# Weight sums of the next layer's projection: other queues, an earlier place, and one part on another engine

## The chip, the core and the metric

The kernel runs on one core of one Trainium2 chip. A core has a matrix engine (TensorE, in the profile PE, its weight loads PEld), three engines for elementwise work (VectorE, DVE; ScalarE, ACT; GpSimd, POOL), and SyncE (SP), which here only issues DMAs. Each of the five works through its own instructions in order; they wait for one another by semaphores. DMAs are issued by SyncE, ScalarE and Pool, each on a queue of its own, and are carried by 16 DMA engines.

The metric is the device time of one execution in microseconds, lower is better. A profiled execution comes with it, whose times are counted from the first instruction.

## What is computed

Two layers, each an attention block and a gated block with layer norms in front; both layers use the same weights. S is 2048 tokens, D is 448 features, 16 heads of 28, F is 1792, all in float32:

```python
def _A_ref(x, wqkv, wo):
    B, S, D = x.shape
    H = 16
    Dh = D // H
    qkv = (lambda x, *d: x.transpose(*d))((x @ wqkv).reshape(B, S, 3, H, Dh), 2, 0, 3, 1, 4)
    q, k, v = qkv[0], qkv[1], qkv[2]
    scores = jnp.einsum("bhqd,bhkd->bhqk", q, k) * (Dh ** -0.5)
    p = _softmax(scores, axis=-1)
    o = jnp.einsum("bhqk,bhkd->bhqd", p, v)
    return (lambda x, *d: x.transpose(*d))(o, 0, 2, 1, 3).reshape(B, S, D) @ wo

def _B_ref(x, w_gate, w_up, w_down):
    g = jnp.einsum("bsd,df->bsf", x, w_gate)
    u = jnp.einsum("bsd,df->bsf", x, w_up)
    h = _sigmoid(g) * u
    return jnp.einsum("bsf,fd->bsd", h, w_down)

x = A_x
x = x + _A_ref(_layernorm(x, axis=-1), A_wqkv, A_wo)
x = x + _B_ref(_layernorm(x, axis=-1), B_w_gate, B_w_up, B_w_down)
x = x + _A_ref(_layernorm(x, axis=-1), A_wqkv, A_wo)
x = x + _B_ref(_layernorm(x, axis=-1), B_w_gate, B_w_up, B_w_down)
```

## The kernel before

Tokens are worked on in four blocks of 512. Products are made in float16 with every operand split in a high and a low part, so that three products (high by high, high by low, low by high) stand for one in float32. The high part is a scaled copy, the low part the rest, and the two parts of an activation are usually made by ScalarE (high) and VectorE (low).

**What the weight sums are for.** From the second layer on, part of the query and key projection is made by a scheme with fewer multiplications. It needs sums and differences of 2 x 2 sub-blocks of the weights. These are made once, during the first layer, kept in device memory (`qs_parts`), and loaded again at the end of the first layer. The columns of the query and key weights are 7 tiles of 128; three pairs of them, `PAIRS_QK = ((0, 1), (4, 5), (2, 6))`, are treated this way. For each pair there are two steps:

- `read_pair(j, queue)` (L725) reads the pair's columns with four DMAs (for each of the two tiles one of 384 rows and one of 64 rows, L731 and L732) into half of a tile `raws`, and has Pool zero the rows left over (L733). Pairs 0 and 1 share one `raws`.
- `keep_pair(j)` (L738) makes the sums: `add_up` (L246, L254) four additions on VectorE; `split_sums` (L257) then four high parts, on ScalarE (L263) or, if it is handed VectorE, there (L261), and six low parts on VectorE (L266), into a tile `pack`; Pool then writes it to `qs_parts` by a DMA (L748). Where the two tiles of the pair have different scales (pair 2), VectorE scales both first (L744).

**Storage.** Tiles in fast memory come from a list of 19 slots (`big`) that is first in, first out: `get` takes the slot free the longest, `put` hands one back at the end. A new tile waits until the last work on its slot's previous tile is done, a DMA included. A second list (`qrt`, 12 slots) holds the small ones.

**The first layer's projection** (`project`, L823). For each block, `qk` makes the seven query and key tiles: 11 matmuls each (L618) into one of four rotating banks; ScalarE makes the high part (L868), VectorE the low part (L869), ScalarE the squares (L871), VectorE the first step of their maximum (L875), and SyncE writes both parts to device memory (L878). The product that adds up the squares of a head (L847, L850) is issued three tiles late. After the eviction of tile i comes whatever stands in `fill[i]`. After the seven tiles, `vals` makes four value products (L643 to L641), evicted by ScalarE (L1119); `after[j]` is called before the eviction of value tile j.

The blocks' normalised rows go through device memory to be transposed: `squares` (L362, L379) on VectorE, `store` (L391, four DMAs on SyncE), `gather` (L399, L401, SyncE, which waits until the store has landed), then `ready` (L222 ScalarE, L223 VectorE) splits the gathered features in two parts. `tell.add` (L1297) measures other weights on VectorE during blocks 2 and 3.

Pair 0 is read on SyncE's queue during the value products of block 1, after block 3's gather, and kept in `fill[0]` of block 2. Pair 1 is read on SyncE's queue in `fill[0]` of block 3, and kept at the end of `guard_of_norms` (L1215), which is called during the value products of block 2 and prepares the bound for the softmax. Then comes a branch on that bound (L1241) and the attention.

**Attention and what follows.** `attend` (L1495) runs some 450 us with TensorE, ScalarE and VectorE together; pair 2 is read near its end on Pool's queue (`along`). `out_project` (L1683) multiplies with `wo`: after the products of six token tiles VectorE does `keep_pair(2)`, then adds the first four results to x (L1709) and takes their statistics (L549, L550). Pool makes the factor of the norm from them (L552, L554), VectorE scales the rows with it (L362), TensorE turns them (L562). Ahead of this, ScalarE issues four DMAs, loads the table of the next function (L1685) and then makes pair 2's high parts.

Of the kernel before, what the change touches and what calls it, by code (L numbers as in the profile page):

```python
# [121 lines left out]
def interleaved_layers(ctx: ExitStack, tc: tile.TileContext, x_in, wqkv, wo, w_gate, w_up,  # L122
                       w_down, out):
    nc = tc.nc
# [29 lines left out]
    def bank(i, name):  # L154
        return psum(f"bank{i}", name, [P, 512])
# [101 lines left out]
    def split_sums(t, v, by, engine=None):  # L257

        def high(to, a):
            if engine is nc.vector:  # L260
                nc.vector.tensor_scalar(to, a, by, None, op0=ALU.mult)  # L261
            else:
                nc.scalar.activation(to, a, AF.Copy, scale=by)  # L263

        def low(to, hi, a):
            nc.vector.scalar_tensor_tensor(to, a, by[0:hi.shape[0]], hi, op0=ALU.mult,  # L266
                                           op1=ALU.subtract)

        sums = add_up(v)
        s12, s34 = [a.rearrange("p a k n -> p (a k) n") for a in sums]  # L270
        for to, a in ((t[:, 0:2], v[:, 0:2, 0]), (t[:, 2:6], s12), (t[:, 6:10], s34),
                      (t[:, 10:14].rearrange("p (k z) n -> p k z n", k=2), v[:, 2:4])):
            high(to, a)
        for to, hi, a in ((t[:, 14:16], t[:, 0:2], v[:, 0:2, 0]),
                          (t[:, 16:20], t[:, 2:6], s12),
                          (t[:, 20:23], t[:, 6:9], s34[:, 0:3]),
                          (t[:, 23:25], t[:, 10:12], v[:, 2])):
            low(to, hi, a)
        low(t[64:P, 9], t[0:64, 9], s34[0:64, 3])
        low(t[64:P, 12:14], t[0:64, 12:14], v[0:64, 3])  # L280
        qrt.put(*sums)
# [373 lines left out]
    class WeightsQKV:  # L655
# [79 lines left out]
        def pair(self, j):  # L735
            return self.raws[:, j % 2].rearrange("p (s z n) -> p s z n", s=4, z=2)

        def keep_pair(self, j):  # L738
            v, t = self.pair(j), big.get("pack", [P, N_SUMS, P], F16)
            m = [int(i > ALONE) for i in PAIRS_QK[j]]  # L740
            by = up[:, m[0]:m[0] + 1]
            if m[0] != m[1]:
                for z in range(2):
                    nc.vector.tensor_scalar(v[:, :, z], v[:, :, z], up[:, m[z]:m[z] + 1], None,  # L744
                                            op0=ALU.mult)
                by = ones[:, 0:1]
            split_sums(t, v, by)
            nc.gpsimd.dma_start(qs_parts[j], t)  # L748
            big.put(t)
            if j > 0:  # L750
                big.put(self.raws)
# [71 lines left out]
    def project(layer, wq, begun):  # L823
# [4 lines left out]
        def ones_of_values():  # L828
            for v in values:
                nc.gpsimd.memset(v[:, :, :, DH:VC], 0.0)  # L830
                nc.gpsimd.memset(v[:, :, :, DH:DH + 1], 1.0)
# [313 lines left out]
        blks = begun + [Block(b, layer == 1, True) for b in range(len(begun), NB)]  # L1145
        idle = None
        sq = lambda b, *js: lambda: blks[b].squares(js)
        b1, b2, b3 = blks[1:]
        if layer == 0:
# [12 lines left out]
            fill = [idle, idle, lambda: b1.norm([0, 1]), lambda: b1.norm([2, 3]), idle, scaled]  # L1162
# [5 lines left out]
        if layer == 0:  # L1168
            fin = qk(0, blks[0], fill, None)
            vals(0, blks[0], along_values)  # L1170
            fill = [b2.gather, b3.norm, sq(3, 0, 1), sq(3, 2, 3), idle,
                    lambda: b2.ready(0, 1), lambda: (b2.ready(2, 3), b3.store())]
            fin = qk(1, b1, fill, None)
            vals(1, b1, {0: b3.gather, 1: lambda: wq.read_pair(0), 2: fin})
            add = tell.add
            fin = qk(2, b2, [lambda: wq.keep_pair(0),
                             lambda: b3.ready(0, 1), lambda: b3.ready(2, 3), idle, add, add,
                             add], None)
            fin = qk(3, blks[3], [lambda: (add(), wq.read_pair(1)), add, add], fin)
        else:  # L1180
            ones_of_values()
            wq.load_usual()
            h2, h3, s3 = b2.half_steps(), b3.half_steps(), b3.squared()
            ready = [lambda kt=kt: b1.ready(kt) for kt in range(4)]
            both = lambda *steps: lambda: [do() for do in steps]
            fin = qk_sums(0, blks[0], {0: ready[0:1], 1: ready[1:2], 2: s3[0:1],
                                       4: ready[2:3], 5: ready[3:4] + s3[1:2]})
            vals(0, blks[0], {0: both(s3[2], s3[3], s3[6], h2[0]), 1: both(s3[4], s3[7]),
                              2: both(fin, s3[5], s3[8], s3[9], b3.store),
                              3: both(h2[1], h2[2], b3.gather)})  # L1190
            fin = qk(1, b1, h2[3:10], None)
            big.put(*wq.qk)
            vals(1, b1, {0: both(*h3[0:2]), 1: both(h3[2], fin), 2: both(*h3[3:5]),
                         3: h3[5]}, banks=(3, 0, 1, 6))
            fin = qk_sums(2, b2, {0: h3[6:7], 1: h3[7:8], 3: h3[8:9], 4: h3[9:10]}, None, True)
            fin = qk_sums(3, b3, {}, fin)
# [18 lines left out]
        def guard_of_norms():  # L1215

            fin()
            heads[0].load()
            nc.vector.tensor_reduce(top, peaks, axis=AX.X, op=ALU.max)
            nc.vector.scalar_tensor_tensor(bnd, top[:, 0:1], SLACK, top[:, 1:2], op0=ALU.mult,  # L1220
                                           op1=ALU.mult)
            nc.gpsimd.tensor_tensor(bnd, bnd, half[0:H, 0:1], op=ALU.pow)
            nc.vector.tensor_scalar(guard, zero, bnd, -1.0 / UNIT, op0=ALU.add, op1=ALU.mult)
            nc.gpsimd.dma_start(g_scr[:, 0, :], guard)
            nc.gpsimd.dma_start(g_scr[:, 1, :], zero)
            big.put(guard, zero)
            if layer == 0:
                wq.keep_pair(1)

        def worst_of_heads():  # L1230
            pb = bank(4, "bounds")
            nc.tensor.matmul(pb[0:1, 0:H], bnd, ident[0:H, 0:H], start=True, stop=True)
# [450 lines left out]
    def out_project(outs, gate, wq):  # L1683
        new_banks()
        nc.scalar.activation(warm, warm, AF.Sigmoid)  # L1685
        nc.scalar.reg_load(gate_scale, back.bitcast(I32)[0:1, 3:4])
        first, second = Block(0, True), Block(1, True)
        steps = deque([first.turn_raw] + first.half_steps())
        early = second.squared()[:TB + TB // 2]
        pms = {}  # L1690

        def products(ts, banks):
            for t, i in zip(ts, banks):
                pms[t] = bank(i, "op")[:, 0:D]
                by_tokens(pms[t], outs.hi(t), outs.lo(t), None, gate.out, range(3))

        def tails(ts):


            for t in ts:  # L1700
                nc.tensor.matmul(pms[t], outs.tail(t), gate.out[:, 0, 3, :], start=False,  # L1701
                                 stop=False)
            for i, t in enumerate(ts):
                r = slice(64 * (i % 2), 64 * (i % 2) + 64)
                nc.tensor.matmul(pms[t], outs.tail(t, i % 2), gate.out[r, 1, 3, :], start=False,  # L1705
                                 stop=True)

        def add(t):
            nc.vector.scalar_tensor_tensor(x[:, t, :], pms[t], back[:, 1:2], x[:, t, :],  # L1709
                                           op0=ALU.mult, op1=ALU.add)  # L1710

        gate.load_gu()
        gate.load_usual()
        products(range(6), range(6))
        if wq:
            wq.keep_pair(2)
        first.begin()
        tails(range(4))
        for t in range(4):
            add(t)  # L1720
            first.stats(t)
        products((6, 7), (6, 7))
        tails(range(4, 8))
        for t in range(4, 8):
            add(t)
        for t in range(4):
            first.scale(t)
        products((8, 9), (0, 1))
        products((10,), (6,))
        run_fill(steps)  # L1730
        for do in early[:2]:
            do()
        products((11,), (7,))
        run_fill(steps, 2)
        tails(range(8, 12))
        for t in range(8, 12):
            add(t)
        for do in early[2:]:
            do()
        products((12, 13), (2, 3))  # L1740
        run_fill(steps, 4)
        products((14, 15), (0, 1))
        run_fill(steps, 9)
        tails(range(12, NT))
        for t in range(12, NT):
            add(t)
        big.put(*outs.kt, gate.out)
        return first, second
# [425 lines left out]
    wq = WeightsQKV()  # L2174
# [44 lines left out]
    for layer in range(LAYERS):  # L2219
# [4 lines left out]
        wq = WeightsQKV()  # L2224
# [30 lines left out]
```

## Time and profile before

| | |
|---|---|
| three runs, us | 1907.41, 1908.41, 1908.43 |
| median of the runs | 1908.41 us |
| the profiled execution's own time | 1906.35 us |
| its span, first to last instruction | 1904.6 us |
| mean granted clock of TensorE | 0.997 |
| data moved by DMA | 278.71 MB |

In the profile's timelines a row is: start in us, length in us, engine, line of the kernel, operation, output <- inputs, shapes, how many instructions are merged in the row, and in brackets how long the engine stood idle before it and what ended that. `SPq`, `ACTq`, `POOLq` and `DVEq` are the queues' own instructions, such as issuing a DMA. In a view of waits a row has the total in us, the number of times, and the longest. In a view of one source line a row has the least, median and longest duration in ns, and the first and last start. In a view by windows a row has the stretch, then for each engine its busy time, then the granted clock, the busy share of the DMA engines and what they moved in GB/s.

### The profile page before, as it was taken

Reading aid. Unit: us, or ns where it says so; the run is one execution under the profiler, and the core shown is the slowest. Engines: PE = TensorE matmul, PEld = TensorE weight load, DVE = VectorE, ACT = ScalarE, POOL = GpSimd, SP = SyncE. Lnnn points to the kernel's source line nnn. Section 1 sums busy time; section 2 is a strip of 40 time slices with the busy share of each in tenths; the row PEclk is TensorE's granted clock in tenths of the full one; section 3 lists DMA queues with packets and bytes.
Section 4 is the critical chain, followed back from the end, with each engine's and each line's share of the span. In section 5 each row is a group of like instructions: output and inputs, shape, how many; then the busy total and the mean of one; then the engine's idle time right before and its main releaser. Section 6 shows DMA issues by size and latency. Waiting matters only on the chain. (4 is left out here: it accounts for less than half of the span.)

```text
span 1904.6 us, 57187 instructions
## 1 busy us (share of the span) xinstructions
PE 1883.3 (99%) x24531; PEld 1365.9 (72%) x24531; DVE 1479.3 (78%) x2984; ACT 1424.6 (75%) x1885; POOL 248.8 (13%) x481
## 2 busy tenths in 40 slices
PE   9899999999999999999999999999999999999999
PEld 4446755556554899999987565687656668999998
DVE  7668989898987887777867577787787688877664
ACT  5459999999993665555547799999999746555541
POOL 3123112122201111212110000000000021111110
PEclk9999999999999999999999999999999999999999
DMA  7666434434332755556583421221120246566553
GB/s 249 205 196 191 141 108 137 115 113 131 109 116 82 239 195 212 213 205 224 195 254 117 117 51 29 49 51 40 38 52 13 74 151 229 198 230 223 215 207 141
DMA packets 118872, 278.71 MB, mean 146 GB/s; under 512 B 14574, under 2 KB 74478, under 8 KB 118480
## 3 DMA queue, kind: packets, MB, share of 16 engines
q0 software_dynamic: 33296, 165.13, 24.0%
q1 hardware_dynamic: 84160, 108.45, 20.1%
q8 instruction: 194, 3.18, 0.7%
q10 hardware_dynamic: 1152, 1.38, 0.3%
q14 instruction: 70, 0.57, 0.1%
HBM read 213.43 MB, written 53.08 MB: 140 GB/s over the span
## 5 line engine op out<-in xcount | busy, mean ns | idle before, releaser
L1538 ACT ACTIVATE prob_s<-sc 128x1536 f32<-128x1536 f32 (+1 forms) x657 | 888.2, 1483 | 8.9 <-PE sc L1523 8.0
L1574 PE MATMUL acc<-prob_s,val_s 128*32 128x256 f32 (+3 forms) x7700 | 574.8, 384 | 0.2 <-issue 0.2
L1523 PE MATMUL sc<-qp_s 114*32 114x512 f16 x7868 | 557.8, 379 | 0.1
L633 PEld LDWEIGHTS <-gu_s 128*128 128x128 f16 x4368 | 426.7, 98 | 45.9 <-PE op L1705 0.7
L1523 PEld LDWEIGHTS <-qp_s 114*32 114x32 f16 x8192 | 282.1, 96 | 195.3 <-issue 83.3
L1574 PEld LDWEIGHTS acc<-prob_s,val_s 128*32 128x32 f32 x7700 | 283.1, 110 | 132.1 <-issue 12.3
L633 PE MATMUL chain<-xwide_s,gu_s 128*128 128x256 f16 x2016 | 247.6, 273 | 0.0
L1887 PE MATMUL dnp<-dn_s,hparts_s 128*128 128x224 f16 x2184 | 246.0, 259 | 0.3 <-DVE x L1905 0.3
L1887 PEld LDWEIGHTS <-hparts_s 128*128 128x128 f16 x2184 | 210.2, 98 | 5.6 <-issue 0.5
L1554 DVE SCALAR_TENSOR_TENSOR power_q<-power_q,expo_q 128x512 f32<-128x512 f32 x243 | 168.2, 692 | 8.3
L1960 ACT COPY one_q<-chain 128x256 f32<-128x256 f32 x224 | 82.3, 372 | 113.2 <-PE chain L633 112.6
L1976 DVE TENSOR_TENSOR one_q<-side,one_q 128x512 f32<-128x512 f32 x112 | 72.2, 686 | 96.5 <-PE side L633 96.4
L633 PE MATMUL side<-xshort_s,gu_s 128*128 128x256 f16 x1120 | 140.6, 273 | 0.0
L1768 POOL DMA_DIRECT2D gu_s<-gu_parts x104 | 56.2, 541 | 427.4 <-PE side L633 426.0
L1605 DVE STREAM_TRANSPOSE oturned_q<-acc 128x512 f32<-128x512 f32 x32 | 23.0, 717 | 98.4 <-PE acc L1574 98.3
L1840 ACT CAST hparts_s<-hsums_q 128x256 f16<-128x256 f32 (+1 forms) x152 | 71.5, 484 | 36.6 <-DVE hsums_q L1852 23.0
L1574 PE MATMUL acc<-power_q,val_s 128*32 128x256 f32 (+3 forms) x300 | 94.2, 396 | 0.0
L633 PE MATMUL side<-xwide_s,gu_s 128*128 128x256 f16 x672 | 91.7, 273 | 0.0
L618 PE MATMUL qkp<-xhl_s,wqk_s 128*128 128x512 f16 x385 | 88.9, 386 | 0.9 <-ACT wqk_s L235 0.6
L1987 ACT ACTIVATE one_q<-one_q 128x512 f32<-128x512 f32 x56 | 35.3, 630 | 65.2 <-DVE one_q L1976 64.9
L1548 DVE TENSOR_SCALAR expo_q<-aside,base 128x512 f32<-128x512 f32 x81 | 60.6, 748 | 21.8 <-PE aside L1523 21.5
L1844 DVE TENSOR_TENSOR hparts_s<-hsums_q,hparts_s 128x256 f16<-128x256 f32 (+1 forms) x152 | 72.7, 517 | 5.9 <-ACT hparts_s L1840 5.9
(262 smaller groups left out, 2398.1 us busy)
## 6 DMA issues: line engine op xcount, KB each, us to landing
gu_s<-gu_parts POOLq DMA_DIRECT2D x104, 800.0 KB, 5.9
dn_s<-dn_parts POOLq DMA_DIRECT2D x42, 784.0 KB, 7.5
qp_s<-qk_scr SPq DMA_DIRECT2D x96, 224.0 KB
gu_parts<-pack_s POOLq DMA_DIRECT2D x14, 800.0 KB, 3.8
xt_scr<-xs_s SPq DMA_DIRECT2D x48, 224.0 KB
xraw_s<-xt_scr SPq DMA_DIRECT2D x12, 768.0 KB
qk_scr<-qkhl_q SPq DMA_DIRECT2D x35, 256.0 KB
qp_s<-qk_scr SPq DMA_DIRECT2D x64, 112.0 KB
```

The lines of the kernel that those rows point to most:

```text
L618: nc.tensor.matmul(pm, w, x, start=(i == 0), stop=(i == len(terms) - 1))
L633: nc.tensor.matmul(pm, a, x, start=(first and i == 0), stop=(i == len(terms) - 1), skip_group_check=True)
L1523: nc.tensor.matmul(ps[32 * j:32 * j + 32, :], hd.k[:, keys], hd.q[:, qb * W:(qb + 1) * W], start=True, stop=True, tile_position=(0, 32 * j))
L1538: nc.scalar.activation(prob[:, 0:n, :], ps[:, 0:n, :], AF.Exp, scale=exp_scale)
L1548: nc.vector.tensor_scalar(y, ps, base2[:, 0:1], -126.0, op0=ALU.mult, op1=ALU.max)
L1554: nc.vector.scalar_tensor_tensor(p, p, c[k], y, op0=ALU.add, op1=ALU.mult)
L1574: nc.tensor.matmul(acc[qb * VC:(qb + 1) * VC, s], v[:, kc % TB, h, :], probs[c * NB + qb][:, s], start=(kc == 0 and a == 0), stop=(kc == N ...
L1840: nc.scalar.copy(to[:, :, 0], a)
L1844: nc.vector.tensor_tensor(to[:, :, 1], a, to[:, :, 0], op=ALU.subtract)
L1887: nc.tensor.matmul(pm, a[:, x, t], w[:, p, y], start=(begin and n == 0 and (j == 0 or alone)), stop=(n == 2), skip_group_check=True)
L1960: nc.scalar.copy(to, pm)
L1976: nc.vector.tensor_tensor(one[m], side[m], one[m], op=ALU.add)
```

## The change

Pair 0 is read on Pool's queue in `fill[2]` of block 1, between the two halves of block 3's `squares`; pair 1 on ScalarE's queue at the second value tile of block 1, where pair 0 was read. Pair 0 is kept before the first tile of block 2, pair 1 after it. The read of pair 1 in block 3 and its keeping in `guard_of_norms` are gone. Pair 2 is kept where it was, and its high parts are made by VectorE.

```diff
-        def keep_pair(self, j):
+        def keep_pair(self, j, engine=None):
...
-            split_sums(t, v, by)
+            split_sums(t, v, by, engine)
...
-            fill = [b2.gather, b3.norm, sq(3, 0, 1), sq(3, 2, 3), idle,
+            fill = [b2.gather, b3.norm,
+                    lambda: (b3.squares([0, 1]), wq.read_pair(0, nc.gpsimd)), sq(3, 2, 3), idle,
                     lambda: b2.ready(0, 1), lambda: (b2.ready(2, 3), b3.store())]
             fin = qk(1, b1, fill, None)
-            vals(1, b1, {0: b3.gather, 1: lambda: wq.read_pair(0), 2: fin})
+            vals(1, b1, {0: b3.gather, 1: lambda: wq.read_pair(1, nc.scalar), 2: fin})
+            wq.keep_pair(0)
             add = tell.add
-            fin = qk(2, b2, [lambda: wq.keep_pair(0),
+            fin = qk(2, b2, [lambda: wq.keep_pair(1),
                              lambda: b3.ready(0, 1), lambda: b3.ready(2, 3), idle, add, add,
                              add], None)
-            fin = qk(3, blks[3], [lambda: (add(), wq.read_pair(1)), add, add], fin)
+            fin = qk(3, blks[3], [add, add, add], fin)
...
             big.put(guard, zero)
-            if layer == 0:
-                wq.keep_pair(1)
-
         def worst_of_heads():
...
         if wq:
-            wq.keep_pair(2)
+            wq.keep_pair(2, nc.vector)
         first.begin()
```

## The prediction

> **What bounds the kernel.** I read the engine totals first, then what TensorE waited for over the whole run, since an engine that is busy 99% of the span can only be helped where it stands still.
>
> ```profile
> PE 1883.3 (99%) x24531; PEld 1365.9 (72%) x24531; DVE 1479.3 (78%) x2984; ACT 1424.6 (75%) x1885; POOL 248.8 (13%) x481
> ...
> PE qnorm L847 <- DVE sq_q L875: 6.9, 1, 6.9
> PE turn L562 <- DVE xn_s L362: 4.9, 2, 3.6
> PE vp L643 <- DVEq L1241: 1.9, 1, 1.9
> PE op L643 <- DVE x L1709: 0.9, 1, 0.9
> ```
>
> Two places matter: one stall of 6.9 us, and one group of 0.9 + 3.6 us. The change touches the cause of both. The timelines of TensorE, SyncE, ScalarE and VectorE around the first (start, length, engine, line) show it:
>
> ```profile
> 77.46 2.54 PE L618 MATMUL qkp<-xhl_s,wqk_s 128*128 128x512 f16 x11
> 86.90 0.37 PE L847 MATMUL qnorm<-sq_q,ind 128*128 128x256 bf16 x1 [6.90 <-DVE sq_q L875]
> 87.06 4.82 PE L618 MATMUL qkp<-xhl_s,wqk_s 128*128 128x512 f16 x11
> 91.72 0.27 PE L847 MATMUL qnorm<-sq_q,ind 128*128 128x256 bf16 x1
> 111.92 0.35 PE L643 MATMUL vp<-wv_s,xhl_s 128*128 128x448 f16 x1
> ...
> 74.02 0.38 SPq L399 DMA_DIRECT2D xraw_s<-xt_scr  x1
> 74.99 0.58 SPq L731 DMA_DIRECT2D raws_s<-in_A_wqkv_dram  x1
> 76.79 0.50 SPq L732 DMA_DIRECT2D raws_s<-in_A_wqkv_dram  x1
> ...
> 80.60 0.51 ACT L263 ACTIVATE pack_s<-raws_s,up 128x256 f16<-128x256 f32 x1 [8.91 <-DMA raws_s<-in_A_wqkv_dram]
> ...
> 81.63 0.42 DVE L254 TENSOR_TENSOR sums_q<-raws_s 128x256 f32<-128x256 f32 x1 [9.61 <-DMA raws_s<-in_A_wqkv_dram]
> 85.45 0.47 DVE L266 SCALAR_TENSOR_TENSOR pack_s<-raws_s,up,pack_s 64x256 f16<-64x256 f32 x1
> 86.56 0.28 DVE L875 TENSOR_TENSOR sq_q<-sq_q 128x256 bf16<-128x256 bf16 x1
> 88.57 0.28 DVE L875 TENSOR_TENSOR sq_q<-sq_q 128x256 bf16<-128x256 bf16 x1
> 108.52 0.28 DVE L875 TENSOR_TENSOR sq_q<-sq_q 128x256 bf16<-128x256 bf16 x1
> ```
>
> Pair 0 stands on SyncE's queue behind block 3's gather, which waits until block 3's store has landed (74.02). So its read is issued at 74.99 to 77.29 and used from 80.60. ScalarE and VectorE work in order, and the pair's sums stand ahead of the eviction of tile 1 of block 2. Tile 1's squares are ready at 86.84; TensorE had finished tile 4 at 80.00 and needs them for the norm product. After the gap 11 matmuls take 4.82 us and not 2.54. The place costs 6.9 + 2.3 = **9.2 us**.
>
> **The change, first stage.** Pair 0's four issues go to Pool's queue during block 1, pair 1's four to ScalarE's queue; both pairs' sums then stand around tile 0 of block 2, and guard_of_norms and SyncE's queue lose pair 1. I followed the first-in-first-out slot list through the code: pair 0 takes the slot of block 2's transposed rows, free when their store has landed, which is also what releases SyncE's gather at 57.16; pair 0 is issued then, with nothing behind it on Pool's queue but its own pack's write, and is there long before its use near 68. SyncE's queue gets rid of 2 x 2.3 us of issues, which brings block 2's and 3's stores of queries and keys forward; nothing waited for those.
>
> ```profile
> 57.16 0.38 SPq L399 DMA_DIRECT2D xraw_s<-xt_scr  x1
> ...
> 62.55 1.14 ACT L222 CAST xhl_s<-xraw_s 128x512 f16<-128x512 f32 x2 [4.60 <-DMA xraw_s<-xt_scr]
> 65.78 1.39 ACT L1119 ACTIVATE val_s<-vp 128x448 f32<-128x448 f32 x3
> ...
> 65.02 0.28 DVE L875 TENSOR_TENSOR sq_q<-sq_q 128x256 bf16<-128x256 bf16 x1
> 67.17 0.40 DVE L889 TENSOR_REDUCE peaks<-knorm 16x1 f32<-16x256 f32 x1
> ...
> 65.45 0.49 PE L850 MATMUL knorm<-sq_q,ind 128*128 128x256 bf16 x3
> ...
> L263 ACT ACTIVATE pack_s<-raws_s,up x4: 507/606/707, 80.6 to 118.9; 128x256 f16<-128x256 f32 x2, 128x512 f16<-128x512 f32 x2
> L263 ACT ACTIVATE pack_s<-sums_q,up x4: 722/722/723, 82.5 to 118.2; 128x512 f16<-128x512 f32 x4
> ```
>
> *ScalarE.* First eviction of block 1's values done at 66.25; four issues at SyncE's price (74.99 to 77.29: 2.3 us) to 68.55; three evictions of 0.46 to 69.95; pair 0's four high parts, 0.51 + 2 x 0.72 + 0.71 = 2.7, to 72.6. Behind the issues wait only those evictions, whose banks TensorE wants again from about 70.3.
>
> *VectorE.* Idle from 67.57, so pair 0's four adds are hidden by ScalarE's evictions (1.7 at 0.42 each, were they not); three lows of up to 0.47 follow the last high part, to about 73.9. Tile 0's low part and squares take 0.9 (85.92 to 86.84): 74.8. Pair 1: 81.63 to 85.92 is 4.3, and tile 1 0.9 more: **80.0**, just when it is needed. ScalarE's part of pair 1 fits beside it if the second pack, which takes the slot of block 3's transposed rows, is free by about 75.2; before, that store had landed at 74.0. Behind a wait for it on ScalarE tile 1's eviction would be queued, and behind that TensorE.
>
> *Tile 2.* It stands behind the first two casts of block 3's gather: 74.02 plus 57.16 to 62.55 (5.4) is 79.4, plus 62.55 to 65.30 (2.75) is 82.15. TensorE needs it after tile 5, 82.45. From there to the first values product TensorE took 20.2 us without a stop (91.72 to 111.92), and VectorE from tile 2 (88.85) to the fourth tile of block 3 (108.80) took 19.95, just as fast. So the whole 9.2 us can be won, and the loss is by how much tile 2 comes later than 82.45.
>
> What can make it later is not in the trace: a read of 448 rows x 256 columns x 4 bytes, 0.46 MB, beside the transfers on this chain.
>
> ```profile
> 60.00:62.00 2.00, 2.00 (x12) 1.02 (x11) 1.98 (x5) 0.00 (x0) 0.31 (x1) 1.00 1.05 337
> 68.00:70.00 2.00, 2.00 (x11) 0.88 (x9) 0.00 (x0) 0.54 (x1) 0.00 (x0) 1.00 0.94 182
> ...
> qs_parts<-pack_s POOLq DMA_DIRECT2D x1, 800.0 KB, 8.3
> ```
>
> In these windows the last two numbers are the share of the DMA engines and GB/s. Both are full. Pair 0 beside block 2's gather: 0 to 0.46 MB / 337 GB/s = 1.4 us, and TensorE waits for it at 65.45, 0.15 us after the squares. Pair 1 beside block 3's store: 0 to 0.46 / 182 = 2.5. Pair 0's pack (0.82 MB) written while block 3's gather is read: 0 to 2.4. Together 0 to 6.3; the last row shows Pool's write waiting behind other queues (8.3 us to landing at 590.8), so I charge the two Pool transfers 0.4 each and pair 1, on a hardware queue, half: 1.2. Tile 2 is at 84.15, the loss 1.7, the gain **7.5** (bounds 3.2 and 9.2). Pair 1's removal from guard_of_norms is worth nothing by itself: no TensorE wait of the list falls there but the branch's 1.9, which the bound and not the pair leads to.
>
> [...]
>
> **Second stage: pair 2's high parts by VectorE, in out_project.**
>
> ```profile
> 582.89 0.42 DVE L254 TENSOR_TENSOR sums_q<-raws_s,sums_q 128x256 f32<-128x256 f32 x1
> 587.16 0.48 DVE L266 SCALAR_TENSOR_TENSOR pack_s<-raws_s,ones,pack_s 128x256 f16<-128x256 f32 x1 [3.85 <-ACT pack_s L263]
> 590.27 0.68 DVE L1709 SCALAR_TENSOR_TENSOR x<-op,back,x 128x448 f32<-128x448 f32 x1
> ...
> 590.79 0.56 POOL L748 DMA_DIRECT2D qs_parts<-pack_s  x1 [43.59 <-issue]
> 602.02 0.18 POOL L552 TENSOR_SCALAR rs<-mv 128x1 f32<-128x1 f32 x1 [10.66 <-issue]
> ...
> L552 POOLq MODIFY_POOL_CONFIG  x2: 37/37/37, 591.4 to 591.5; - x2
> L1432 POOLq MODIFY_POOL_CONFIG  x2: 37/37/37, 188.9 to 188.9; - x2
> L1432 POOL PARTITION_ALL_REDUCE size<-sums x1: 1125/1125/1125, 195.4 to 195.4; - x1
> L261 DVE TENSOR_SCALAR pack_s<-raws_s,up x28: 345/414/484, 325.6 to 536.6; 128x256 f16<-128x256 f32 x14, 128x512 f16<-128x512 f32 x14
> L261 DVE TENSOR_SCALAR pack_s<-sums_q,up x28: 478/480/486, 325.8 to 536.2; 128x512 f16<-128x512 f32 x28
> ```
>
> VectorE waits 3.85 us for ScalarE. Its own high parts take 0.35 + 2 x 0.48 + 0.48 = 1.8, so from 583.31 to 585.1, the lows (3.1) to 588.2 and not 590.23: 2.1 earlier. Behind the last low stand the adds to x (TensorE's 0.9 us wait goes) and Pool's write; behind that Pool changes its configuration and starts its first statistic 11.2 us after the write's issue. Pool's four steps pace TensorE's turn, so the gain is what Pool gains. At the same 11.2 that is **2.1**. It is 0 if Pool's restart hangs on the end of the other transfers, and at most 6.1 if the change of configuration costs 6.5, as at 188.9 to 195.4, and not the 10.5 of 591.5 to 602.02 (2.1 + 4.0, more than the 0.9 + 3.6 that TensorE waits there, since its transposes are paced too). I take the row of the same place, 11.2.
>
> [...]
>
> **Sum.** 7.5 + 2.1 = 9.6 off the profiled execution's 1906.35 is 1896.75. Its median of runs is 2.06 higher (1908.41), so **1898.8**. Everything later moves along, as TensorE is busy throughout.
>
> **Rivals.** *The transfers collide fully:* the gain is 3.2 + 2.1 = 5.3, 1903.1. For it, the two full windows; against it, the gaps beside them. 0.17. *Pool restarts in 6.5 us:* 7.5 + 6.1, 1894.8; for it 188.9, against it the same event at 591.5. 0.10. *Slower, pair 1 lands late:* the stall of before returns with two pairs in front of tile 1. Tile 1's squares come 5.2 after the landing (81.63 to 86.84), so TensorE loses landing - 74.8, plus 2.3 of slow matmuls; 11.3 is used up at a landing of 83.8, 17.5 us after the first issue at 66.3. Landing at 87 gives 3.2 over before, 1911.6. Pair 0 took 6.6 from issue to use. 0.07. *The gain is swallowed at the branch before attention* (the 1.9 us wait), if transfers and not TensorE end that wait: only 2.1 stays, 1906.3. Against it: that wait is short, with SyncE's queue moving up too. 0.07. The forecast keeps 0.59.
>
> A difference under 0.2% (3.8 us) can't be told from none. The forecast, the short restart and three quarters of the collisions are faster: 0.82; the branch and the rest of the collisions same: 0.10; slower 0.08 with what I overlook. The range, 1894 to 1905, takes in the full collision and the short restart, and leaves out the last two rivals.
>
> **What would show it.** Right: the 6.9 us wait at L847 shrinks below 2 us, no run of doubled matmuls after it, ScalarE never waits for raws, values of block 2 start near 104; later VectorE starts the adds near 588.7 and Pool its statistic near 600. Wrong: a TensorE wait at L850 near 65.5, a ScalarE wait on the second pack, a late gather, or ScalarE waiting for pair 1.

## The result, and the profile after

| us | before | changed |
|---|---|---|
| median of six runs each | 1908.42 (1907.41 to 1909.96) | 1896.75 (1893.97 to 1898.73) |
| span of the profiled execution | 1904.6 | 1894.1 |
| to block 2's first values product | 111.92 | 104.08 |
| from there to the first score (branch) | 17.27 | 15.53 |
| attention, to the last head's transpose | 448.07 | 449.31 |
| from there to the first turn of rows (`out_project`) | 26.23 | 24.05 |
| the rest of the span | 1301.1 | 1301.1 |

The ratio is 0.9939, 95% interval 0.9926 to 0.9951: 11.7 us of the medians, 10.5 us of the two profiled executions. The table splits the 10.5: 7.8 in the first stage, 1.7 at the branch, 1.2 given back in attention, 2.2 in `out_project`.

The engine totals, from the page of the changed kernel:

```profile
PE 1881.7 (99%) x24531; PEld 1435.6 (76%) x24531; DVE 1480.4 (78%) x2988; ACT 1422.9 (75%) x1881; POOL 250.9 (13%) x485
```

What its TensorE waited for, over the whole run (total, times, longest):

```profile
PE turn L562 <- DVE xn_s L362: 3.7, 2, 2.6
PE acc L1573 <- issue: 0.9, 1, 0.9
PE qnorm L847 <- DVE sq_q L875: 0.7, 1, 0.7
```

The wait at L847 fell from 6.9 to 0.7, the branch's 1.9 and the adds' 0.9 are gone from the list, and of the longest wait of `out_project`, 3.6, there are 2.6 left. The totals say nothing of this: TensorE is at 99% in both.

The first place in the changed kernel's timelines of TensorE, SyncE, Pool, ScalarE and VectorE:

```profile
80.22 2.54 PE L618 MATMUL qkp<-xhl_s,wqk_s 128*128 128x512 f16 x11
83.44 0.27 PE L847 MATMUL qnorm<-sq_q,ind 128*128 128x256 bf16 x1 [0.69 <-DVE sq_q L875]
83.55 2.54 PE L618 MATMUL qkp<-xhl_s,wqk_s 128*128 128x512 f16 x11
104.08 0.35 PE L643 MATMUL vp<-wv_s,xhl_s 128*128 128x448 f16 x1
...
73.68 0.38 SPq L399 DMA_DIRECT2D xraw_s<-xt_scr  x1
...
57.79 0.79 POOL L731 DMA_DIRECT2D raws_s<-in_A_wqkv_dram  x1 [2.64 <-DMA xt_scr<-xs_s]
...
65.17 0.38 ACTq L731 DMA_DIRECT2D raws_s<-in_A_wqkv_dram  x1
66.83 0.62 ACTq L732 DMA_DIRECT2D raws_s<-in_A_wqkv_dram  x1
67.49 1.42 ACT L1119 ACTIVATE val_s<-vp 128x448 f32<-128x448 f32 x3 [0.46 <-issue]
68.78 0.52 ACT L263 ACTIVATE pack_s<-raws_s,up 128x256 f16<-128x256 f32 x1
73.63 0.51 ACT L263 ACTIVATE pack_s<-raws_s,up 128x256 f16<-128x256 f32 x1 [1.36 <-DMA xt_scr<-xs_s]
80.64 1.14 ACT L222 CAST xhl_s<-xraw_s 128x512 f16<-128x512 f32 x2 [3.26 <-DMA xraw_s<-xt_scr]
...
78.25 0.28 DVE L875 TENSOR_TENSOR sq_q<-sq_q 128x256 bf16<-128x256 bf16 x1
83.11 0.28 DVE L875 TENSOR_TENSOR sq_q<-sq_q 128x256 bf16<-128x256 bf16 x1
```

Neither pair is waited for: at 68.78 and 73.63 no bracket names `raws`. What ScalarE waits for at 73.63 is the slot of the second pack, that is block 3's store, and this is hidden: tile 1's squares are ready at 78.53 and used after 80.11. What is late in its place is the gather of block 3, read from 73.68 and cast from 80.64; tile 2 stands behind it and costs 0.69. The 11 matmuls behind that short gap take 2.54 and not 4.82.

Further on, the timelines of VectorE, Pool and TensorE in `out_project`:

```profile
580.29 0.68 DVE L1708 SCALAR_TENSOR_TENSOR x<-op,back,x 128x448 f32<-128x448 f32 x1 [1.13 <-PE op L1704]
...
579.46 0.56 POOL L748 DMA_DIRECT2D qs_parts<-pack_s  x1 [41.02 <-DVE pack_s L266]
591.50 0.18 POOL L552 TENSOR_SCALAR rs<-mv 128x1 f32<-128x1 f32 x1 [11.48 <-issue]
...
592.97 4.03 PE L562 MATMUL turn<-ident,xn_s 128*128 128x128 f32 x16 [2.56 <-DVE xn_s L362]
```

And the change of Pool's configuration there, from the view of line 552 (least, median, longest in ns, first and last start in us):

```profile
L552 POOLq MODIFY_POOL_CONFIG  x2: 37/37/37, 580.1 to 580.1; - x2
```

Attention ended 8.34 earlier (577.26 against 568.92). On the time axis of before, Pool's write is therefore issued 3.0 earlier and its first statistic comes 2.2 earlier. In between lie 12.0 us now and 11.2 before: Pool gave 0.8 back.

### The profile page after: what moved, and what is told of

Same layout as the page of the kernel before. It is cut to its first block, busy times and chain, and to the rows that moved or that the text cites. A ratio compares the mean times of both kernels' runs of the same rounds, so it can differ in the third digit from the quotient of the medians.

```text
span 1894.1 us, 57178 instructions
## 1 busy us (share of the span) xinstructions
PE 1881.7 (99%) x24531; PEld 1435.6 (76%) x24531; DVE 1480.4 (78%) x2988; ACT 1422.9 (75%) x1881; POOL 250.9 (13%) x485
## 5 line engine op out<-in xcount | busy, mean ns | idle before, releaser
L1573 PE MATMUL acc<-prob_s,val_s 128*32 128x256 f32 (+3 forms) x7700 | 595.9, 384 | 0.9 <-issue 0.9
L1522 PE MATMUL sc<-qp_s 114*32 114x512 f16 x7868 | 578.5, 379 | 0.2 <-DMA qp_s<-qk_scr 0.2
L1522 PEld LDWEIGHTS <-qp_s 114*32 114x32 f16 x8192 | 316.1, 96 | 166.6 <-issue 64.2
L1573 PEld LDWEIGHTS acc<-prob_s,val_s 128*32 128x32 f32 x7700 | 327.3, 110 | 91.4 <-issue 8.7
L1573 PE MATMUL acc<-power_q,val_s 128*32 128x256 f32 (+3 forms) x300 | 94.2, 396 | 0.0
```

The lines of the kernel that those rows point to most:

```text
L1522: nc.tensor.matmul(ps[32 * j:32 * j + 32, :], hd.k[:, keys], hd.q[:, qb * W:(qb + 1) * W], start=True, stop=True, tile_position=(0, 32 * j))
L1573: nc.tensor.matmul(acc[qb * VC:(qb + 1) * VC, s], v[:, kc % TB, h, :], probs[c * NB + qb][:, s], start=(kc == 0 and a == 0), stop=(kc == N ...
```

## The experiments

All ratios are to the kernel before, in runs on the same chip.

**The change in two halves.** The first kernel is the changed one with pair 2's high parts on ScalarE again; the second is the kernel before with only these on VectorE.

```diff
-            wq.keep_pair(2, nc.vector)
+            wq.keep_pair(2)
...
-            wq.keep_pair(2)
+            wq.keep_pair(2, nc.vector)
```

> The first stage alone: pair 2's high parts are back on ScalarE, the reads and the earlier sums of pairs 0 and 1 stay. Theory (the two stages are independent and each sets a wait of TensorE by itself): the profile's span falls by 8.3 us, from 1904.6 to about 1896.3; TensorE's 6.9 us wait at L847 is gone and the wait for the turn is 3.6 again, the wait at L643 for the adds 0.9. Rival (the second stage pays only because VectorE's and Pool's queues stand otherwise after the first): the span stays within 1 us of the changed kernel's 1894.1.

> The second stage alone, on the kernel before: only pair 2's high parts by VectorE. Theory: Pool's write is issued about 2.5 us earlier and its first statistic of out_project starts about 2.2 us earlier, the span falls by 2.2 us to about 1902.4, and the 6.9 us wait at L847 is as before. Rival (Pool's restart hangs on the end of all transfers there): Pool starts no earlier than before, relative to the end of attention, and the span falls by less than 0.5 us.

The reads and the earlier place alone: 1900.95 us, ratio 0.9958 (0.9941 to 0.9974); 102.94 to the values, 15.53 at the branch, 26.55 in `out_project`. VectorE alone: 1904.97, ratio 0.9976 (0.9966 to 0.9985); 111.82, 17.27 and 21.85. Its waits:

```profile
PE qnorm L847 <- DVE sq_q L875: 6.5, 1, 6.5
PE turn L562 <- DVE xn_s L362: 2.5, 5, 0.9
PE vp L643 <- DVEq L1241: 1.9, 1, 1.9
```

The gains, 8.6 and 4.6, add up to the whole within their intervals, and each half moves the waits of its own stage. The spans of the two executions, 1898.2 (1896.3 expected) and 1902.6, show this less well: the part behind `out_project` was 3.0 us (1304.1) and 1.7 us (1302.8) longer in them than before. Over all the executions here it lies between 1298.5 and 1305.9; what makes that spread was not tested. The branch belongs to the first half. In the second half Pool needed only 9.85 us from its write's issue (588.43) to the statistic (598.28), so the 11.2 of before is no constant.

**Which of the two pairs matters, and which queue.** To the kernel before only the early read of pair 0 was added; and in the changed kernel pair 1 was put back on SyncE's queue, at its new place.

```diff
             fill = [b2.gather, b3.norm,
+                    lambda: (b3.squares([0, 1]), wq.read_pair(0, nc.gpsimd)), sq(3, 2, 3), idle,
...
-            vals(1, b1, {0: b3.gather, 1: lambda: wq.read_pair(0), 2: fin})
+            vals(1, b1, {0: b3.gather, 2: fin})
...
-            vals(1, b1, {0: b3.gather, 1: lambda: wq.read_pair(1, nc.scalar), 2: fin})
+            vals(1, b1, {0: b3.gather, 1: lambda: wq.read_pair(1), 2: fin})
```

> Of the first stage only pair 0's read is moved to Pool's queue in block 1; its sums stay in fill[0] of block 2, and pair 1 is read in block 3 and kept in guard_of_norms as before. Theory (the 6.9 us were the late landing of pair 0, not the place of its sums): tile 1's squares are ready near 77, TensorE's wait at L847 falls below 1 us, the values of block 2 start near 103.5 and the span falls by 8 us or a little more up to there; the branch's wait of 1.9 us at L643 stays, so the whole falls by 7 to 8.5. Rival (the sums in front of tile 1 cost the time wherever the data are): more than 3 us of the wait stay.

> The changed kernel, with pair 1 read on SyncE's queue at the same place of the program, behind block 3's gather. Theory: SyncE's queue stands still until block 3's store has landed (gather issued at 73.7 in the changed kernel), so pair 1 is issued near 74 to 76 and lands near 80 to 82; its sums stand ahead of tile 1's on ScalarE and VectorE, the wait at the norm product returns with 6 to 9 us, block 2's values start near 111 to 113, and the span is 7 to 9 us above 1894.1. Rival: only pair 0's early landing matters and the queue of pair 1 does not; then block 2's values start within 1 us of 104.1 and the span within 2 us of 1894.1.

Pair 0 early: 1900.65, ratio 0.9951 (0.9935 to 0.9968), values of block 2 at 103.13. No wait at L847 is left, and the branch's 1.9 stays. Pair 0 alone thus has the whole gain of the first stage (8.8 us), and its median is no worse than the 1900.95 of both reads: the 1.7 at the branch is seen in the stages and not in these medians. (Its span, 1900.4, fell by 4.2 and not by 7 to 8.5; the part behind `out_project` was 4.5 longer in this execution.)

Pair 1 on SyncE's queue: 1905.90, ratio 0.9981 (0.9972 to 0.9991), values at 112.79, 8.7 later than in the changed kernel; the span, 1903.8, lies 9.7 above, 0.7 more than expected. SyncE, ScalarE and TensorE there:

```profile
74.58 1.16 SPq L731 DMA_DIRECT2D raws_s<-in_A_wqkv_dram  x1
...
81.90 0.51 ACT L263 ACTIVATE pack_s<-raws_s,up 128x256 f16<-128x256 f32 x1 [9.58 <-DMA raws_s<-in_A_wqkv_dram]
...
88.33 0.37 PE L847 MATMUL qnorm<-sq_q,ind 128*128 128x256 bf16 x1 [8.00 <-DVE sq_q L875]
```

The whole first-stage gain is thus the removal of one late landing in front of tile 1. Pair 1 moved in front of that tile is free only because its read has a queue that doesn't stand still behind block 3's gather: four issues at 65.17 instead of 74.58 are worth the 8.7 us. What is saved in this run is a wait in a queue; the four issues themselves take 2.3 us (65.17 to 67.45 in the changed kernel).

**Is the gather late because pair 0's pack is written beside it?** In the version of the next experiment, the statement that writes pair 0 stands behind pair 1's sums, which was meant to hold the write back.

```diff
+            if j == 0:
+                self.kept = t
+                return
+            if j == 1:
+                nc.gpsimd.dma_start(qs_parts[0], self.kept)
+                big.put(self.kept)
```

> The kernel with pair 2's pack written by ScalarE's queue (span 1887.6), and also with pair 0's write to device memory issued only behind pair 1's sums. Theory: pair 0's write beside block 3's gather made that land 1.5 us late (6.96 us from issue to first use, 5.4 at block 2); with the write gone from there the gather takes 5.4 to 6 us, the wait of 0.7 us at tile 2's norm product goes, and block 2's values start at 102.7 to 103.5 (103.35 in the execution it starts from, 104.1 in the changed kernel). Two writes are then closer to the branch: the wait of 1.9 us may come back. In all between -1 and +1.5 us against 1887.6. Rival: the gather is slow for another reason (block 2's stores of queries and keys); then it still takes 7 us.

1891.36, ratio 0.9911 (0.9895 to 0.9928), against 0.9902 (0.9884 to 0.9919) without this edit: no difference. But the edit did not hold the write back. Pool had nothing else to do, waited only for the last of pair 0's sums, and issued the write at 72.64, as without the edit:

```profile
72.64 0.58 POOL L752 DMA_DIRECT2D qs_parts<-pack_s  x1 [11.78 <-DVE pack_s L266]
```

The gather takes 6.6 us to its first cast (73.22 to 79.82) with the edit and 6.7 (73.24 to 79.91) without it, beside the same write. So this run doesn't answer the question. All the executions together say more. In ten, this one included, pair 0 is read early and the gather's first cast doesn't wait for a late pair 1:

| pair 0's write against the gather's issue | executions | gather's issue to first cast, us |
|---|---|---|
| 0.6 to 0.9 us ahead | 6, the changed kernel and this run among them | 6.3 to 8.2 |
| 0.4 to 3.2 us behind | 4 | 5.3 to 5.7 |

So pair 0's write is the likely cause of the late gather, when it gets ahead of it. It is not shown: no run holds the write back by an edit, and the order came out by itself. The longest is in the run with the sooner write below, where the write was issued at 74.30:

```profile
74.97 0.38 SPq L399 DMA_DIRECT2D xraw_s<-xt_scr  x1
...
83.17 1.14 ACT L222 CAST xhl_s<-xraw_s 128x512 f16<-128x512 f32 x2 [4.54 <-DMA xraw_s<-xt_scr]
...
85.97 0.27 PE L850 MATMUL qnorm<-sq_q,ind 128*128 128x256 bf16 x1 [1.97 <-DVE sq_q L878]
```

Here the late gather costs TensorE 1.97.

**What Pool waits for in `out_project`.** In the kernel before the first statistic came 2.9 us after Pool's own write had landed, in the changed one 3.1 (and 3.1 to 3.3 in three of the runs above, where the landing took 6.6 to 8.3 us). The theory was that Pool waits for its own write. First the write was given to ScalarE's queue.

```diff
-            nc.gpsimd.dma_start(qs_parts[j], t)
+            (nc.scalar if j == 2 else nc.gpsimd).dma_start(qs_parts[j], t)
```

> The changed kernel with pair 2's pack written by ScalarE's queue, not Pool's. Theory (Pool changes its configuration only behind its own write and then waits for that write to land): the change of configuration runs right after Pool's last read, near 550, Pool starts its first statistic when VectorE has it, near 582, and TensorE's wait of 2.6 us for the turn is gone; with the transposes no longer paced by Pool the span falls by 4 to 6 us, to 1888 to 1890. Rival (the restart costs its 10 us whatever stands before it, or hangs on the transfers of SyncE there): Pool starts near 591 again and the span stays within 1 us of 1894.1.

1889.83, ratio 0.9902 (0.9884 to 0.9919), span 1887.6: below both kernels. The timeline of Pool:

```profile
580.91 0.19 POOL L552 TENSOR_SCALAR rs<-mv 128x1 f32<-128x1 f32 x1 [43.61 <-DVE mv L550]
```

The view of line 552 in this run:

```profile
L552 POOLq MODIFY_POOL_CONFIG  x2: 37/37/37, 537.3 to 537.3; - x2
```

Pool takes the statistic 0.18 us after VectorE's, and `out_project` falls from 24.05 to 21.33. But the last row shows that more has changed than the wait: without a DMA of Pool between, the change of configuration is made 43 us earlier, beside attention. So this run can't say how long the change takes, or why. Two runs leave Pool a small write of 32 KB, the rest going to SyncE's queue: the first of the 25 sums, which is ready early, and then the one that is ready last.

```diff
-            nc.gpsimd.dma_start(qs_parts[j], t)
+                nc.gpsimd.dma_start(qs_parts[j, :, 0:1], t[:, 0:1])
+                nc.sync.dma_start(qs_parts[j, :, 1:], t[:, 1:])
```

> The changed kernel, with only the first of pair 2's 25 sums written by Pool's DMA and the other 24 by SyncE's queue. Theory: Pool's change of configuration waits until Pool's own write has landed, and takes some 3 us more (2.9 to 3.3 us in the five executions so far). A write of 32 KB should land in 3 to 5 us and not in 8.9, so the first statistic is forecast at 579.5 + 4 + 3, about 586 to 588 (591.5 in the changed kernel), and the span 3 to 5 us under 1894.1. Rival A: a fixed 11 to 12 us from the issue of any DMA of Pool: the statistic stays near 591 and the span within 1 us of 1894.1. Rival B: Pool waits for all traffic, whoever issued it: the same as A here, with the statistic 3 us after the big write's landing.

1891.21, ratio 0.9906 (0.9890 to 0.9923). Pool's timeline:

```profile
575.62 0.61 POOL L749 DMA_DIRECT2D qs_parts<-pack_s  x1 [37.12 <-DVE pack_s L261]
583.92 0.18 POOL L552 TENSOR_SCALAR rs<-mv 128x1 f32<-128x1 f32 x1 [7.70 <-DVE mv L550]
```

Its small write in the view of the DMA issues (last the median us from issue to landing), then the view of line 552, then the windows of this run (the last two numbers are the share of the DMA engines and GB/s):

```profile
qs_parts<-pack_s POOLq DMA_DIRECT2D x1, 32.0 KB, 2.1
```

```profile
L552 POOLq MODIFY_POOL_CONFIG  x2: 37/37/37, 576.3 to 576.3; - x2
```

```profile
576.00:578.00 2.00, 2.00 (x13) 0.99 (x12) 2.00 (x5) 1.00 (x1) 0.23 (x1) 1.00 0.59 136
578.00:580.00 2.00, 2.00 (x13) 0.90 (x13) 1.23 (x4) 0.48 (x2) 0.00 (x0) 1.00 0.16 35
580.00:582.00 2.00, 2.00 (x14) 0.90 (x14) 1.55 (x4) 0.00 (x0) 0.00 (x0) 1.00 0.73 190
```

The wait for Pool shrank, and `out_project` took 21.32 us, as with ScalarE's write (the span, 1892.0, lies 2.1 and not 3 to 5 below the changed kernel's; the first projection began 1.6 us later in this execution, 13.36 against 11.79). But the theory doesn't fit. The write left 4 us earlier than expected, when its one sum was ready, and had landed at 577.7; 3 us more is 580.7, yet the statistic, whose input was there at 581.94, came at 583.92: 6.2 after the landing and 7.6 after the change of configuration. Both rivals fall too: 583.92 is 8.3 and not 11 after the issue, and it comes before SyncE's write is even issued (586.48). So with the other sum:

> The changed kernel; of pair 2's 25 sums Pool writes only the 14th, the one that VectorE finishes last, so that Pool's small write (32 KB) is issued near 579.5 as the whole one was, and the change of configuration follows at about 580.1, when SyncE's loads fill the DMA engines; SyncE writes the other 24 behind those loads. Reading 1 (Pool waits for its own write to land and takes 3 us more): the small write lands in 2 to 4 us, the first statistic is at 585 to 587. [...]

1897.84, ratio 0.9944 (0.9922 to 0.9965), span 1894.4. The same four views:

```profile
579.55 0.56 POOL L749 DMA_DIRECT2D qs_parts<-pack_s  x1 [41.01 <-DVE pack_s L266]
590.84 0.18 POOL L552 TENSOR_SCALAR rs<-mv 128x1 f32<-128x1 f32 x1 [10.72 <-issue]
```

```profile
qs_parts<-pack_s POOLq DMA_DIRECT2D x1, 32.0 KB, 1.7
```

```profile
L552 POOLq MODIFY_POOL_CONFIG  x2: 37/37/37, 580.2 to 580.2; - x2
```

```profile
582.00:584.00 2.00, 2.00 (x12) 1.08 (x11) 1.90 (x4) 0.00 (x0) 0.00 (x0) 1.00 0.94 355
584.00:586.00 2.00, 2.00 (x14) 0.72 (x12) 1.93 (x4) 0.00 (x0) 0.00 (x0) 1.00 0.98 371
586.00:588.00 2.00, 2.00 (x12) 1.07 (x11) 1.97 (x6) 0.00 (x0) 0.00 (x0) 1.00 1.04 350
588.00:590.00 2.00, 2.00 (x13) 1.01 (x11) 0.64 (x2) 0.00 (x0) 0.00 (x0) 1.00 0.99 356
```

The write has landed at 581.3, and Pool stands for 9.6 us more. So a wait for its own write doesn't make this time. (Behind the whole write, the statistic follows the landing by 2.9 to 3.7 us in all ten executions that have it; that Pool waits for it there as well isn't excluded.) What the two runs leave is the stretch from the change of configuration itself: 7.6 us from change to statistic where the DMA engines were busy by 0.59, 0.16 and 0.73 in the first 6 us, 10.6 where SyncE's loads filled them (0.94 to 1.04 from 582 to 590). But how full they are doesn't set the time alone. The run with the write at the branch, below, has the `out_project` of the changed kernel; its change of configuration came at 580.0, the DMA engines were busy by 0.91 to 1.05 from 580 to 590, and the statistic came after 8.5 us:

```profile
588.45 0.18 POOL L552 TENSOR_SCALAR rs<-mv 128x1 f32<-128x1 f32 x1 [8.57 <-DVE x L1716]
```

In the eleven executions with a late DMA of Pool and the change beside these loads it is 8.5 to 11.6 us. What makes that spread was not tested, nor by what way the loads would lengthen the stretch. The 6.5 us of the kernel before at 188.9 don't speak against such a lengthening: there the DMA engines were busy by 0.70 and 0.87 up to 192 and idle to 194 (share 0.00).

**The branch.** Before, VectorE came to its semaphore instruction behind the branch (L1241) at 126.9, after the compare at 122.0; TensorE waited 1.9 for it. In the changed kernel these are 117.0 and 114.1 (views of that line, of the kernel before and of the changed one):

```profile
L1241 DVEq COMPARE_BRANCH  x2: 68/70/72, 122.0 to 1062.2; - x2
L1241 DVEq EVENT_SEMAPHORE  x2: 21/21/21, 126.9 to 1066.0; - x2
```

```profile
L1240 DVEq COMPARE_BRANCH  x2: 68/70/72, 114.1 to 1051.8; - x2
L1240 DVEq EVENT_SEMAPHORE  x2: 21/21/21, 117.0 to 1055.1; - x2
```

From 4.9 to 2.9 us, with no work of VectorE in between in either. Pair 1's part of `guard_of_norms` is what went from there: its sums, and its write, issued 0.5 us ahead of the compare. Three variants of the changed kernel put the write alone back, at different times; a fourth is the kernel before with the write alone taken behind the branch.

```diff
             big.put(guard, zero)
+            if layer == 0:
+                nc.gpsimd.dma_start(qs_parts[1], wq.kept)
+                big.put(wq.kept)
```

> The changed kernel, with pair 1's sums made where they are, and only the write of them to device memory issued at the end of guard_of_norms, where the kernel before had it. Theory: the 0.8 MB write in flight delays the instructions after the branch; TensorE's wait of 1.9 us at the first values product behind the branch returns, and from block 2's values to the first score it is about 17.3 us (kernel before) and not 15.5. The start of block 2's values stays within 1 us of 104.1. Rival: it was the sums' work of ScalarE and VectorE at that place; then the wait stays away and the stretch stays at 15.5 us.

> The changed kernel, with the write of pair 1's sums held back until VectorE has the branch's value: it is issued about 10 us after block 2's first values product (9.6 us in the kernel before, 6.2 us in the run with the write at the end of guard_of_norms), so it fills the DMA engines while the engines take the branch. Theory: the write delays what VectorE needs behind the branch; the wait of 1.9 us returns, and from block 2's values to the first score it is 17.0 to 17.6 us. Rival: the sums' own work in guard_of_norms made the wait; it stays away and the stretch is 15.5 us.

In the second and third, the write stands in `worst_of_heads`, behind a small step of Pool that reads its result and is no part of the computation (0.56 us long in the second, 0.25 in the third, shown here):

```diff
+                nc.gpsimd.tensor_scalar(half[0:1, 7:8], worst, 0.0, None, op0=ALU.mult)
+                nc.gpsimd.dma_start(qs_parts[1], wq.kept)
```

> As the run with the write held back to the branch, but with a shorter step of Pool ahead of the write, so that it is issued about 0.5 us before VectorE's compare of the branch (121.51 against 122.0 in the kernel before; 113.05 against 113.1 in that run). Theory: the write's descriptors must stand ahead of what VectorE needs behind the branch; now they do, VectorE's semaphore instruction behind the branch comes 4.5 to 5 us after the compare (4.9 in the kernel before, 2.9 in the changed kernel, 3.2 in that run), and the stretch from block 2's values to the first score is 17.0 to 17.6 us. Rival (the sums' work in guard_of_norms): about 3 us and 15.5 us as before.

> The kernel before, with pair 1's sums where they are, and only their write issued behind the branch. Theory (the write delays VectorE at the branch): VectorE's semaphore instruction comes about 3 us after the compare, the wait of 1.9 us goes, and from block 2's values to the first score it is 15.5 us; the span falls by 1 to 2 us against 1904.6. Rival (the sums' instructions ahead of the branch): 4.9 us after the compare, the wait stays and the stretch is 17.3 us.

| write of pair 1's sums | issue against compare, us | compare to semaphore, us | values to first score, us |
|---|---|---|---|
| kernel before | -0.5 | 4.9 | 17.27 |
| end of `guard_of_norms`, sums elsewhere | -3.9 | 3.0 | 15.53 |
| in `worst_of_heads`, sums elsewhere | 0.0 | 3.2 | 15.53 |
| in `worst_of_heads`, sooner, sums elsewhere | -0.3 | 3.3 | 15.58 |
| kernel before, write behind the branch | +0.7 | 3.1 | 15.53 |

The view of the branch's line in the last of these:

```profile
L1245 DVEq COMPARE_BRANCH  x2: 68/70/72, 123.4 to 1065.6; - x2
L1245 DVEq EVENT_SEMAPHORE  x2: 21/21/21, 126.5 to 1069.4; - x2
```

With the sums where they were and only the write moved, the wait is gone (one execution, against three with the write in place, all with 1.9). So the sums alone don't make it, and the rival falls. But the write alone doesn't bring it back either: 0.2 us of waiting at the sooner place, none at the others. The write at its old place is needed for the wait; put back at other times it is not enough for it.

The traces show what stands in between. Their DMA view lists packets that it calls `instruction`. In the first 2.8 us behind the compare (122.0 to 124.8) the kernel before has none of them, but 140 packets of Pool's queue, `software_dynamic`, which are the write; the two `instruction` packets of queue 14 come in the next 2 us. In the changed kernel they come within the first 2.8 us (114.1 to 116.9). The three lines, in this order, give packets, MB and the share of the 16 engines:

```profile
q0 software_dynamic: 140, 0.81, 74.3%
...
q14 instruction: 2, 0.02, 1.9%
...
q14 instruction: 2, 0.02, 1.8%
```

In the three executions with the write at its old place the first of these packets starts 2.9 us after the compare; in all eleven others it starts after 1.0 to 1.2, and VectorE comes to its semaphore after 2.9 to 3.3. At the sooner place one of the two packets starts after 1.2 us, ahead of most of the write, and the other after 3.1. So the write most likely delays these packets, and in these fourteen executions it did so only where it got ahead of them. That fits the time of the write and needs no part of the sums; but that VectorE waits for them is inferred from the times alone, the trace doesn't say which engine a packet is for, and a write another 0.2 us earlier, with the sums elsewhere, was not run. (The first variant's time was 1897.96, ratio 0.9939, 0.9921 to 0.9957, as the changed kernel's. The three others have one execution each: 1893.32, 1899.32 and 1910.41, the last beside 1907.17 for the kernel before. The expected fall of its span did not show: against the profile of before it lost 1.4 up to the values, 1.6 in attention, 0.3 in `out_project` and 2.5 behind it, and won 1.7 at the branch.)

## Why the prediction was right, step by step

**The sum.** For the profiled execution 9.6 us were forecast and 10.55 came (1906.35 to 1895.80): 0.3 and 0.1 more at the two places, 1.7 at the branch, less 1.2 in attention. The rest of the distance from 1898.8 to 1896.75 is the step from the profiled execution to the median: 2.06 was taken over from the kernel before, and it was 0.95.

**Place 1.** The forecast gain was 7.5, the profiled one 7.84, with the values at 104.08 ("near 104"); 0.24 of it is an earlier start of the first projection (11.79 against 12.03). The mechanism held: one late landing in front of tile 1 made the stall. The size held by luck, since terms inside the sum were off with opposite signs. ScalarE's four issues were charged 2.3 us; they run on its queue from 65.17 to 67.45 beside its casts and evictions, and cost it 0.46 idle. Hence pair 0's high parts start at 68.78 and not 69.95, and tile 1's squares are ready at 78.53 and not 80.0. The gather was expected without neighbours at 79.4 and came at 80.64. The 1.2 us that I had charged to pair 1, for delaying block 3's store, did not come: the gather was issued at 73.68 and not later than 74.02. It was the gather that took longer, 6.96 us and not 5.4, with pair 0's write issued 0.63 ahead of it. That write was charged with 0.4, a quarter of what it cost if it is the cause. Tile 2's squares came at 83.39, forecast 84.15. Two of the signs of failure were there: the late gather, which cost 0.69, and the wait for the second pack's slot (1.36), which was hidden.

**"Worth nothing by itself"** was the step that failed: pair 1's leaving `guard_of_norms` gave 1.74 at the branch. I had put that wait down to the bound and had not asked what Pool's write does just ahead of the branch; the run with the write behind the branch shows that it is needed for the wait, and in the traces it stands ahead of the `instruction` packets.

**"Everything later moves along"** held for the rest of the span in this pair of executions (1301.1 in both, out of a spread of 1298.5 to 1305.9), and not quite for attention, which took 1.24 longer. 0.7 of it is TensorE's wait called "issue" at L1573, 0.9 against 0.2; with VectorE's half of the change alone, which touches nothing ahead of attention's end, it was 0.9 too, and over all executions attention took 448.1 to 450.2. So the 1.24 is no larger than the spread between executions; what makes that spread was not tested.

**Place 2.** 2.1 was forecast and 2.18 came, at 588.6 for the adds and 599.8 for the statistic on the time axis of before (588.7 and 600 forecast). The size was right by two errors that happened to cancel: VectorE finished 2.7 and not 2.1 earlier (its high and low parts overlap a little more than their durations added up), and the 11.2 us from the write's issue, which I took over as a constant, became 12.0. The small early write and the one of the last sum point to the change of configuration as what stands in between: 7.6 us in the one, 10.6 in the other, 11.4 in the changed kernel (580.1 to 591.50). The rival with 6.5 us named what could be won there, 4.0 on top: with the change of configuration made early, the two stretches from the end of attention to the first gated chain took 4.9 us less than in the changed kernel (21.33 + 12.94 against 24.05 + 15.07).

**Rivals.** Full collision meant 6.0 us lost at tile 2: TensorE waited 0.7 there, and 2.0 in the worst execution. Pair 1 landing late is exactly what its queue avoids; on SyncE's queue it happened. The swallowed gain at the branch went the other way.

## What to carry to other kernels

Pair 1's read, standing behind a waiting gather in SyncE's queue, was issued at 74.58 and not 65.17, and the values came 8.7 us later: where a read is late by such a wait, try a queue with nothing in front before asking what bandwidth it costs. Check an engine's queue of DMA issues separately from its compute: here four issues of 2.3 us beside ScalarE's work cost it 0.46 us, while one DMA of Pool moved a change of configuration from 537.3 to 580.1, to the worst moment. When a stall has a constant-looking length, change what surrounds it before taking the length over: a release time that followed a landing by 2.9 to 3.7 us in ten executions came 9.6 us after it once the write was small. And look in the trace whether an edit moved what it was meant to move: a write that was put later in the program was issued at the same 72.64.

## What the runs showed of the hardware that was not expected

- In these runs Pool's change of configuration stood right behind Pool's previous instruction, whether the statistic was near or not: behind the last write at 580.1 in the changed kernel, and behind a memset at 537.3, 43 us before the statistic, when the last write goes to ScalarE's queue. From it to the first statistic passed 7.6 us where the DMA engines were partly free (0.59, 0.16 and 0.73), and 8.5 to 11.6 in the eleven executions with the change beside SyncE's loads (0.94 to 1.04 from 582 to 590 in the one of 10.6).
- A write issued by Pool 0.5 us ahead of a branch took part in a delay of 2.0 us of VectorE behind it (4.9 against 2.9 to 3.3 us from compare to semaphore): the `instruction` packets behind the branch start 2.9 us after the compare and not 1.0 to 1.2. Issued 0.3 us ahead of it, later, or 3.9 us earlier, it made 0.2 us or nothing of waiting.
- The same gather, in the same place, took 6.3 to 8.2 us from issue to first use where pair 0's write of 0.8 MB was issued 0.6 to 0.9 us ahead of it, and 5.3 to 5.7 where it was issued behind it.
